# Three extra eight-row loads into unused buffers, early in a two-part decode-attention kernel

## The chip, the cores and the metric

The kernel runs on one core of a Trainium2 chip. The metric is device time in microseconds of one execution. Six executions of the kernel before took 1369.67 to 1370.08 us, with a median of 1369.79. One further execution was recorded by the hardware profiler; it took 1369.97 us, and its span, from its first to its last instruction, is 1368.20 us.

## The reference: what is computed

Two attention layers for one new token are computed side by side, each with its own input x (4 sequences, 512 wide), caches and weights, all in bf16. A uses 8 key/value heads for 32 query heads and only the last 2048 positions of its cache; B has 32 heads of each kind and uses all 8192 positions. The results are put side by side.

```python
q = (x @ wq).reshape(B, Sq, H, Dh).transpose(0, 2, 1, 3)
scores = einsum("bhqd,bhkd->bhqk", q, k) * (Dh ** -0.5)
o = einsum("bhqk,bhkd->bhqd", softmax(scores, axis=-1), v)
out = o.transpose(0, 2, 1, 3).reshape(B, Sq, H * Dh) @ wo
# A: k, v are the last 2048 of 8192 positions, each head used by 4 query heads
# result: concatenate([out_A, out_B], axis=-1)
```

There is one query row per sequence and head, so nearly all of the work is reading the caches: 587 MB come from memory in one execution.

## The kernel before

**Chunks.** The work is cut into 40 chunks. The first 8 belong to A, one per key/value head, with 2 MB of keys and 2 MB of values each. The other 32 belong to B, one per sequence and group of four heads, with 8 MB of keys and 8 MB of values each.

**The big buffer.** `kv` (line 229) holds ten units of 128 rows x 16 KB. While A runs, units 0 and 1 hold A's query weights, 6 and 7 B's query weights (`dma_wq`, line 337), 8 and 9 A's keys, 4 and 5 A's values (`dma_A`, line 361). Units 2 and 3 are used by nothing until B. In B, units 0 to 3 take keys and 4 to 7 values. Units 8 and 9 are a common second half: GpSimd copies the later half of a chunk's keys, and then of its values, there (`spread_copies`, line 369), so that the unit it came from is free for the next load. B's first chunk is an exception: `dma_K` (line 378) loads its keys' second half into units 8 and 9 directly, so units 2 and 3 are first written by the keys of B's second chunk.

**Compute.** TensorE transposes each block of 128 positions of the keys (line 477), VectorE and ScalarE take the transposed blocks out of PSUM into `kt` (lines 547 and 545), TensorE multiplies them with the queries (`sc`, line 479), ScalarE makes the exponentials (line 671), TensorE multiplies these with the values (`po`, line 479), and per chunk the output projection is added into `fin`.

**Order.** Nothing decides the order at run time. A recording object (`_Sched`, line 54) collects for each engine a list of instructions with the results each waits for; `add_dma` (line 78) gives every load a semaphore and a name. SyncE issues all big loads in the order of the lists (lines 457 to 469): query weights of A, first keys of A, query weights of B, then in each turn of A's loop the next keys, the values and a 512 KB block of A's output weights (`dma_wo`, line 346), then B's keys and values chunk by chunk. ScalarE issues the two loads of x (line 335). GpSimd issues no DMA at all; it sets constants, the last of them `back` (lines 312 to 316, named `c_back`), and later runs the copies of line 375.

**Freeing a buffer.** For each of the ten units, the list `held` (line 320) has the names of what must be over before the next load into it may be issued. `take` and `dma_K` read `held` for their waits and set it anew. Before the change, `held[2]` and `held[3]` are empty until B's first entries, so the keys of B's second chunk wait only for the releases of units 0 and 1.

Of the kernel before, what the change touches and what calls it, by code (L numbers as in the profile page):

```python
# [18 lines left out]
NWO = 3  # L19
# [153 lines left out]
def bass_concat_heads__sliding_block_cached__mha_block_cached__decode_kernel(  # L173
# [9 lines left out]
    KC = D // P  # L183
# [4 lines left out]
    WQ = {0: A_wq, 1: B_wq}  # L188
# [30 lines left out]
    sch = _Sched()  # L219
    with ExitStack() as es:  # L220
        block = es.enter_context(nc.Block())

        def sb(name, shape, dt):
            return es.enter_context(nc.sbuf_tensor(name, shape, dt))

        def ps(name, shape, dt):
            return es.enter_context(nc.psum_tensor(name, shape, dt))

        kv = sb("kv", [P, NH, 8192], BF16)
# [42 lines left out]
        semnames = ["eng_pe", "eng_dve", "eng_act", "eng_pool", "eng_sp", "d_x0", "d_x1", "d_o0", "d_o1", "r_k", "r_v", "r_w"]  # L272
        semnames += ["d_h%d" % i for i in range(NH)] + ["d_bk0", "d_bv0", "r_c"]
        semnames += [f + str(i) for f, x in (("d_lk", LASTK), ("d_nk", NEXTK), ("d_fk", HALVES), ("d_lv", LASTV), ("d_nv", NEXTV), ("d_hv", HALVES)) for i in range(len(x))]
        semnames += ["d_wo%d" % i for i in range(NWO)] + ["d_wos"]
        sems = {n: es.enter_context(nc.semaphore(n)) for n in semnames}


# [13 lines left out]
            waits=["c_onesf", "c_identf"], key="c_ind")  # L292
# [27 lines left out]
        held = [[] for _ in range(NH)]  # L320
# [10 lines left out]
        def flat(at, n):  # L331
            return kv[:, at:at + n, :].rearrange("p s x -> p (s x)")

        def dma_x(ab):
            sch.add_dma("act", lambda e: e.dma_start(xs[:, ab, :], X[ab][:, 0, :]), "d_x%d" % ab, key=("x", ab))
# [7 lines left out]
        def wo_slot(g):  # L343
            return g % 2 if g < NCA - 1 else 2

        def dma_wo(g):

            src = A_wo[g * 4 * P:(g + 1) * 4 * P, :].rearrange("(p r) n -> p (r n)", r=4)
            slot = wo_slot(g)
            dst = wor[:, slot, :]  # L350
            sch.add_dma("sp", lambda e: e.dma_start(dst, src), "d_wo%d" % slot,
                        waits=[("fin", g - 2)] if g >= 2 and slot < 2 else [], key=("wo", g))
# [8 lines left out]
        def dma_A(kind, c):  # L361
            ch = chunks[c]
            T = A_k if kind == "k" else A_v
            at = HALF_A[kind][c % 2]
            waits = take((kind, c), at, 1, ("T", ch["s_last"]) if kind == "k" else ("pv", c))
            src = T[:, ch["g"], SkA - W:, :].rearrange("b (pp j) d -> pp b (j d)", pp=P // NB)
            sch.add_dma("sp", lambda e: e.dma_start(kv[:, at, :], src), "d_h%d" % at, waits=waits, key=(kind, c))
# [86 lines left out]
        PIECES_K.update({NC - 5: ("d_fk", HALVES), NC - 4: ("d_fk", HALVES), NC - 3: ("d_fk", HALVES), NC - 2: ("d_nk", NEXTK)})  # L454
        PIECES_V = {NC - 3: ("d_hv", HALVES), NC - 2: ("d_nv", NEXTV), NC - 1: ("d_lv", LASTV)}

        dma_x(0)
        dma_x(1)
        dma_wq(0, 0)
# [2 lines left out]
        for c in range(NCA):  # L462
            if c < NCA - 1:
                dma_A("k", c + 1)
            dma_A("v", c)
            dma_wo(c)
        for c in range(NCA, NC):
            dma_K(c)
            dma_V(c)
# [553 lines left out]
```

## Time and profile before

| what | value |
|---|---|
| median of six executions | 1369.79 us |
| profiled execution, whole | 1369.97 us |
| profiled execution, span | 1368.20 us |
| time outside the span | 1.77 us |
| PE busy | 1198.4 us (88%) |
| VectorE, ScalarE, GpSimd busy | 776.5, 521.1, 470.4 us |
| read from memory | 587.21 MB, 429 GB/s over the span |
| packets of DMA queue 1 | 17432 |

How to read it: busy times are sums over the span and overlap each other. "DMA share" is the mean busy share of the core's 16 DMA engines; by rounding it can exceed 1. A load is cut into packets, which the DMA engines work off one after another, each engine on its own; a load has landed when the last of the engines that carry it is through. The trace holds, for each packet, its queue, start, duration and size, but not its engine, and for each landing signal its time; a 128-row load gives 16 such signals. All times are microseconds from the start of the span unless the text says ns.

### The profile page before, as it was taken

To read this page: it belongs to the slowest core of one execution; us is meant where nothing else is said; L and a number is where in the kernel's file an instruction comes from. 1 tells how busy PE (TensorE), PEld (TensorE's weight loads), DVE (VectorE), ACT (ScalarE), POOL (GpSimd) and SP (SyncE) were. 2 spreads that over 40 slices of the span, in tenths; PEclk is the share of its full clock that TensorE was granted. 3 is DMA by queue.
4 is the path that set the end of the run, shared out by engine and by line. 5 is a ranking of instruction groups with operands and counts; after the bars stand their busy time and mean duration, and the time that the engine had idled before them with its cause. 6 is when DMAs were issued, how large, how long until landed. Compare 5 with 4: busy or idle time off the path is not lost.

```text
span 1368.2 us, 61987 instructions
## 1 busy us (share of the span) xinstructions
PE 1198.4 (88%) x27577; PEld 1130.8 (83%) x27577; DVE 776.5 (57%) x1527; ACT 521.1 (38%) x681; POOL 470.4 (34%) x277
## 2 busy tenths in 40 slices
PE   4898698898989988988889888888998888998998
PEld 4787688887888988887889878888998888997897
DVE  1675455554556555555565655555665555665665
ACT  1553243333334433333344333333443333443443
POOL 2000244334433443344334433443344334432442
PEclk9899899999999999999999999999999999999999
DMA  9999999999999999999999999999999999999998
GB/s 400 426 426 439 433 428 433 429 441 429 429 431 434 436 433 429 435 437 431 433 435 439 425 433 441 435 424 433 443 433 433 425 443 431 433 425 428 426 425 353
DMA packets 17487, 587.54 MB, mean 429 GB/s; under 512 B 1956, under 2 KB 1976, under 8 KB 4408
## 3 DMA queue, kind: packets, MB, share of 16 engines
q1 hardware_dynamic: 17432, 587.21, 99.6%
q8 instruction: 15, 0.25, 0.1%
q14 instruction: 8, 0.07, 0.0%
q10 hardware_dynamic: 32, 0.01, 0.0%
HBM read 587.21 MB, written 0.01 MB: 429 GB/s over the span
## 4 chain that ended last, share of the span: by engine, by line
DMA 62%; PE 33%; DVE 2%; issue 1%; POOL 1%; ACT 0%; SPq 0%; POOLq 0%; DVEq 0%
DMA kv<-in_B_k_cache_dram 53%; PE tr L477 21%; PE sc L479 8%; DMA kv<-in_B_v_cache_dram 7%; PE fin L479 2%; DMA kv<-in_B_wq_dram 2%; POOL kv L375 1%; PE po L479 1%; DVE sA L601 1%; PE ms L479 1%; DVE rm L613 0%; DVE sA L599 0%; ACT pba L711 0%; PE ms L477 0%; DVE zA L802 0%
## 5 line engine op out<-in xcount | busy, mean ns | idle before, releaser
L477 PE MATMUL tr<-identb,kv 128*128 128x128 bf16 x8704 | 696.7, 227 | 110.1 <-POOLq L76 105.7
L375 POOL COPY kv<-kv 128x2048 int32<-128x2048 int32 x248 | 460.5, 1894 | 874.7 <-DMA kv<-in_B_k_cache_dram 308.3
L547 DVE COPY kt<-tr 128x1024 bf16<-128x1024 bf16 x736 | 503.6, 691 | 352.8 <-PE tr L477 350.0
L477 PEld LDWEIGHTS tr<-identb,kv 128*128 128x128 bf16 x8704 | 536.5, 102 | 127.7 <-issue 123.9
L545 ACT ACTIVATE kt<-tr 128x1024 bf16<-128x1024 bf16 x352 | 359.3, 1023 | 716.2 <-PE tr L477 716.0
L479 PE MATMUL sc<-qq,kt 128*128 128x64 bf16 x8192 | 404.5, 193 | 12.6 <-DVE kt L547 9.8
L479 PEld LDWEIGHTS sc<-qq,kt 128*128 128x128 bf16 x8192 | 338.7, 99 | 16.2 <-DVE kt L547 13.1
L479 PE MATMUL po<-pbb,kv 128*128 128x64 bf16 x8192 | 269.1, 194 | 16.7 <-POOLq L76 10.6
L479 PEld LDWEIGHTS po<-pbb,kv 128*128 128x128 bf16 x8192 | 259.5, 99 | 19.4 <-issue 14.0
L671 ACT ACTIVATE pbb<-sc,negb 32x128 bf16<-32x128 f32 x256 | 138.5, 541 | 6.6 <-DVE negb L649 1.8
L818 DVE CAST wor<-tr 128x512 bf16<-128x512 f32 x96 | 62.7, 681 | 0.7 <-PE sc L479 0.7
L617 DVE TENSOR_REDUCE rm<-sc 128x4 f32<-128x512 f32 x64 | 43.9, 686 | 14.3 <-PE sc L479 14.3
L687 DVE TENSOR_REDUCE hs<-pbb 128x4 f32<-128x512 bf16 x64 | 43.9, 686 | 10.4 <-ACT pbb L671 10.4
L683 ACT ACTIVATE hs<-hs 128x4 f32<-128x4 f32 x32 | 6.6, 205 | 105.3 <-DVE hs L679 105.3
L634 DVE TENSOR_REDUCE gm<-ms 4x4 f32<-4x128 f32 x72 | 24.0, 334 | 25.8 <-PE ms L477 25.8
L479 PE MATMUL tr<-wos,back 32*128 32x512 bf16 x384 | 34.5, 383 | 0.0
L479 PE MATMUL sc<-wos,back 32*128 32x512 bf16 x128 | 33.6, 382 | 0.0
L649 DVE TENSOR_SCALAR negb<-ms 128x4 f32<-128x4 f32 x64 | 10.4, 162 | 39.6 <-PE ms L479 39.6
L692 DVE TENSOR_TENSOR fd<-po,hs 128x64 f32<-128x64 f32 x32 | 7.2, 225 | 45.0 <-PE po L479 45.0
L765 DVE TENSOR_TENSOR hs<-ms,hs 128x4 f32<-128x4 f32 x32 | 5.2, 162 | 44.0 <-PE ms L479 44.0
L479 PE MATMUL fin<-wor,oz 128*4 128x256 bf16 x264 | 29.3, 365 | 0.4 <-DVE oz L790 0.4
L479 PE MATMUL sc<-qb,kt 128*128 128x64 bf16 (+3 forms) x512 | 26.1, 196 | 0.2 <-DVE gx L640 0.2
(74 smaller groups left out, 376.4 us busy)
## 6 DMA issues: line engine op xcount, KB each, us to landing
kv<-in_B_k_cache_dram SPq DMA_DIRECT2D x8, 4096.0 KB, 25.7
kv<-in_A_k_cache_dram SPq DMA_DIRECT2D x8, 2048.0 KB, 12.3
kv<-in_A_v_cache_dram SPq DMA_DIRECT2D x8, 2048.0 KB, 13.9
kv<-in_B_v_cache_dram SPq DMA_DIRECT2D x3, 4096.0 KB, 29.1
kv<-in_B_k_cache_dram SPq DMA_DIRECT2D x5, 2048.0 KB, 26.9
kv<-in_B_v_cache_dram SPq DMA_DIRECT2D x4, 2048.0 KB, 27.0
kv<-in_B_k_cache_dram SPq DMA_DIRECT2D x6, 1024.0 KB, 29.8
kv<-in_A_wq_dram SPq DMA_DIRECT2D x1, 4096.0 KB, 12.5
```

Source lines behind the costliest of these rows:

```text
L375: lambda e, x=x: e.tensor_copy(flat(KX, 2)[:, x].bitcast(I32), flat(units, 2)[:, x].bitcast(I32)),
L477: sch.add("pe", lambda e: e.transpose(o, l, r), waits, key)
L479: sch.add("pe", lambda e: e.matmul(o, l, r, start=start, stop=stop), waits, key)
L545: sch.add("act", lambda e: e.activation(dst, src, ACTF.Copy), waits=waits, key=("ev", s))
L547: sch.add("dve", lambda e: e.tensor_copy(dst, src), waits=waits, key=("ev", s))
L601: emit = lambda e, src=src, b=b: e.scalar_tensor_tensor(out=t, in0=src, scalar=mk[:, b:b + 1], in1=t, op0=ALU.mult, op1=ALU.add)
L617: sch.add("dve", lambda e: e.tensor_reduce(out=rm[:, half, :], in_=src, axis=AX.X, op=ALU.max), waits=[("S", ch["s"] + (half + 1) * ch["NG ...
L634: sch.add("dve", lambda e: e.tensor_reduce(out=gm[0:C, m, 0:U], in_=src, axis=AX.XY if B else AX.X, op=ALU.max), waits=[("trm", c, half)], ...
L649: sch.add("dve", lambda e: e.tensor_scalar(out=negb[:, m, 0:C], in0=ms[:, col:col + C], scalar1=-scale, scalar2=None, op0=ALU.mult), waits ...
L671: sch.add("act", lambda e, src=src, dst=dst, pp=pp, u=u: e.activation(dst, src, ACTF.Exp, bias=negb[pp, half, u:u + 1], scale=scale), wait ...
L687: sch.add("dve", lambda e: e.tensor_reduce(out=hs[:, half, :], in_=probs_B(half).rearrange("p j u -> p u j"), axis=AX.X, op=ALU.add), wait ...
L818: sch.add("dve", lambda e: e.tensor_copy(wol[:, u, :], o), waits=[("reord", c) if u == 3 else ("reord", c, u)] + [("fin", prev(c))], key=( ...
```

## The change

A view `probe` of B's query weights is made, 128 rows of 32 KB. Two loads are added to GpSimd's list, behind the last setup instruction, one to SyncE's list, in the turn c = 4 of A's loop, after that turn's block of output weights. Their targets lie in units 2 and 3, in rows that are 4 apart: the first load takes rows 0 to 28 of unit 2 (16 KB each), the second rows 64 to 92 of units 2 and 3 together (32 KB each), the third rows 1 to 29 of half of unit 2 (8 KB each). Nothing reads what they load. `held[2]` and `held[3]` name them, so that the keys of B's second chunk, which overwrite these units, wait for them. Three semaphores are added. Nothing is removed, and the lists of the other engines stay as they were.

```diff
-        semnames += ["d_wo%d" % i for i in range(NWO)] + ["d_wos"]
+        semnames += ["d_wo%d" % i for i in range(NWO)] + ["d_wos", "d_p0", "d_p1", "d_p2"]
...
+        probe = WQ[1].rearrange("(p r) n -> p (r n)", r=KC)
+        sch.add_dma("pool", lambda e: e.dma_start(kv[0:32:4, 2, :], probe[0:8, 0:8192]), "d_p0", waits=[("c_back", 3)], key="p0")
+        sch.add_dma("pool", lambda e: e.dma_start(flat(2, 2)[64:96:4, :], probe[8:16, :]), "d_p1", waits=[("c_back", 3)], key="p1")
+        held[2], held[3] = ["p0", "p1", "p2"], ["p1"]
         dma_x(0)
         dma_x(1)
         dma_wq(0, 0)
...
             dma_A("v", c)
             dma_wo(c)
+            if c == 4:
+                sch.add_dma("sp", lambda e: e.dma_start(kv[1:32:4, 2, 0:4096], probe[16:24, 0:4096]), "d_p2", key="p2")
```

## Prediction

> **What bounds the kernel now.** I read the DMA part of the page first, then a table of stages, then the chain of waits at the end, and last the trace's records of single DMA packets and of landings.
>
> The page's DMA parts:
>
> ```profile
> DMA  9999999999999999999999999999999999999998
> GB/s 400 426 426 439 433 428 433 429 441 429 429 431 434 436 433 429 435 437 431 433 435 439 425 433 441 435 424 433 443 433 433 425 443 431 433 425 428 426 425 353
> ...
> q1 hardware_dynamic: 17432, 587.21, 99.6%
> q8 instruction: 15, 0.25, 0.1%
> q14 instruction: 8, 0.07, 0.0%
> ```
>
> The 16 DMA engines are full in every slice but the last, and queue 1, into which SyncE issues the loads, holds 99.6% of their time. A table of stages says the same with PE beside it (columns: length, then the busy time of PE, PE's weight loads, VectorE, ScalarE and GpSimd, each with its instructions, then PE's clock, DMA share, GB/s):
>
> ```profile
> 68.00:102.00 34.00, 31.08 (x669) 27.49 (x670) 25.38 (x73) 18.59 (x29) 0.00 (x0) 1.00 1.01 428
> 209.70:248.40 38.70, 34.31 (x802) 32.51 (x802) 22.27 (x42) 14.77 (x19) 14.87 (x8) 0.96 1.00 434
> 1340.00:1354.00 14.00, 13.69 (x333) 13.50 (x331) 9.92 (x17) 7.93 (x10) 5.56 (x3) 1.00 1.02 433
> 1354.00:1368.20 14.20, 9.82 (x249) 8.10 (x244) 5.83 (x16) 2.37 (x5) 0.00 (x0) 1.00 0.60 247
> ```
>
> The DMA share is 1.00 while PE has 34.31 us of work in a 38.70 us chunk. The chain of waits over the last microseconds (start, length, what) names what the end hangs on:
>
> ```profile
> 1351.62 0.25 PE sc L479 x8
> 1352.02 0.43 SPq L432
> 1352.50 0.43 SPq L432
> 1352.97 11.44 DMA kv<-in_B_v_cache_dram
> 1364.51 0.42 PE po L479 x8
> 1365.28 0.62 PE fin L479 x8
> 1365.99 0.42 DVE outsb L850
> ```
>
> The last piece of V lands at 1364.41, and 3.8 us of fixed work follow. So the span is "when the slowest of 16 DMA engines is through its bytes", plus 3.8 us. What matters is not the mean engine but the slowest.
>
> The packet records give each engine's pace. A 64 KB packet takes 2.420 us, one of 32 KB 1.213, 16 KB 0.611, 8 KB 0.309, 4 KB 0.159, nearly without spread. The landing records give the order of the engines: in each big load 16 landings are recorded. At 13.35 us the first engine is 0.77 us ahead of the last; at 100.34 seven engines lead by 1.42 to 2.18 us and nine lie within 0.93 of the last; at 212.21 seven lead by 2.92 to 3.74 and seven lie within 0.72; at 1364.41 the first leads by 2.64. The gap does not close by itself, because no engine waits for another. What opens it are the 15 packets of queue 8 (instruction fetches, 16 KB, recorded at 0.98 to 1.11 us each, from 18.6 to 173.2 us): each sets one engine back by about 1 us.
>
> **The change part by part.** It adds three loads and removes nothing; the order on PE, VectorE and ScalarE is the same.
>
> *Load 1* (Pool queue): eight rows of 16 KB. *Load 2* (Pool queue): eight rows of 32 KB. *Load 3* (SyncE): eight rows of 8 KB. In all 448 KB. The nearest row for how rows go to engines is the load of x: four rows of 1 KB each left four 1 KB packets on queue 10, so a row stays whole and goes to one engine. Per engine that is hit: load 1 0.611 us, load 2 1.213, load 3 0.309, by the packet rows above.
>
> GpSimd issues its two after its last setup instruction:
>
> ```profile
> 8.52 2.97 POOL L314 TENSOR_SCALAR_AFFINE_SELECT back<-back 128x512 bf16<-128x512 bf16 x4
> ```
>
> that is at about 11.5 us. Behind them on GpSimd stand only the relays and copies of the B part, whose first busy slice is after 137 us, so GpSimd's own issuing time, which no row shows, is covered by some 120 us. SyncE's load stands between its issues at 78.02 and 78.39:
>
> ```profile
> 78.02 0.33 SPq L351 DMA_DIRECT2D wor<-in_A_wo_dram  x1
> 78.39 0.54 SPq L367 DMA_DIRECT2D kv<-in_A_k_cache_dram  x1
> ```
>
> It delays the K load behind it by one issue, 0.33 to 0.54 us. The engines are then still busy with the load issued at 78.02, which lands at 84.45; a new load's packets start some 2.2 us after its issue (343.46 to 345.7 in the records), so more than 3 us of cover remain. The new wait of the B part's second K load, which SyncE issues at 133.52, is over long before: the first two loads should land before 20 us, the third at about 85. That wait costs nothing; without that cover every load behind it on SyncE would move.
>
> What remains is engine time, and that has no cover on an engine that is already the last. A load that hits the last engine moves the end by its full packet time; on an engine that leads by more than the packet time it costs nothing. So the sum is bounded by 0 below (only leaders are hit) and by 0.611 + 1.213 + 0.309 = 2.13 us above, if the Pool queue's packets run at queue 1's pace. If the 448 KB were spread evenly it would be 28 KB an engine, 1.06 us.
>
> Which engines are hit is the first choice. The trace does not name engines, but it shows which four carry a four-row transfer. At 126.9 us the output of A interrupts four engines; following their packets to 129.3, they lead the last one by about 3.4, 3.4, 2.6 and 2.1 us at 134.49. So four of the engines that a small transfer uses here are leaders. I therefore place load 3 (eight rows, from SyncE) on leaders, at nothing. For the Pool queue no row exists. I take it that the two Pool loads do not both go to the same eight engines, since their target rows (0 to 28 and 64 to 92) lie in different halves of the memory; then one of them hits the last engine. I take the larger, 1.2 us; the smaller would give 0.6.
>
> [...]
>
> The second choice is the pace of the Pool queue. Low end: queue 1's, 0.611 us for 16 KB; queue 14's 8 KB fetches, at 0.307 to 0.325, agree. High end: queue 8's 16 KB packets, up to 1.11 us. I take queue 1's, because it is the only one of these with rows into the same buffers.
>
> [...]
>
> **Sum.** Span 1368.20 + 1.2 = 1369.4. The profiled execution took 1369.97, 1.77 more than its span, and the median is 1369.79, 0.18 less than it: 1369.4 + 1.77 - 0.18 = 1371.0.
>
> **The rivals.**
>
> *Leaders only* (1369.8): all three loads fall on engines that lead. The early leads are 1.42 to 2.18 us, later 2.9 and more, against at most 2.13 us of load. For it: the four known engines lead. Against it: nothing says that Pool's loads use the same ones.
>
> *Piled on the last engines* (1371.9): all three on the half that has the fetches, +2.13. Against it: the four known engines.
>
> *Slower*: the Pool queue's packets run at queue 8's pace because a second queue on a full engine loses its turn: 3 x 1.07 + 0.31 = 3.5 us on the engines that carry all three, 1373.3. It decides once 16 KB cost over 0.81 us there (3 x 0.81 + 0.31 = 2.74 us, which is 0.2%). For it: 15 rows of exactly such a case, a 16 KB packet on another queue beside a full queue 1. Against it: queue 14 does not show it. A first use of the Pool queue may also cost time outside the span, where 1.77 us lie today; no row tells.
>
> *Faster*: setting the leading engines back changes how the engines meet, and the gap shrinks. The most that could bring is the first engine's lead at the end, 2.64 us, and nothing makes the last engine's bytes fewer; I give it -1 us, 1368.8.
>
> **How the numbers follow.** Forecast (one Pool load on the last engine, +0.6 to +1.3) 0.40; leaders only (0 to +0.3) 0.25; piled (+1.8 to +2.1) 0.11; slower (+2.8 to +3.6) 0.22; faster 0.02. A difference under 0.2%, 2.74 us, is about what a measurement of this kernel can tell from no change. The first three cases lie within it: 0.76. The slower case is beyond: 0.22; and 0.02 for faster, at the very most. The first three hold less than 8 in 10, so the range takes in the slower one: 1369.7 to 1373.4.
>
> **What would show it.** In the changed kernel's packet records: 8 packets (or pieces) of 16 and of 32 KB on a new queue from about 12 us, at 0.611 and 1.213 us, or longer for the slower rival. In the landing records after 20 us: the lead of the first engines grows by 1.2 us if the last ones are hit, and shrinks if the leaders are. The last V landing moves by the same amount as the span, and the 3.8 us after it stay. The forecast is wrong if the period of 38.70 us a chunk changes, if GpSimd is late at its first copy, or if the time outside the span grows.

## The result, and the profile after

The changed kernel takes 1373.03 us (median of 20 runs, 1372.66 to 1373.59), the kernel before 1369.83 us (40 runs). The ratio is 1.0023, with a 95% interval of 1.0017 to 1.0029: 3.20 us slower. The forecast was +1.2 us; the time lies in the range, at the place of the slower rival. The profiled execution took 1373.09 us, 1371.4 of them in the span, so the time outside the span stayed at 1.7 us.

The end of the chain of waits, after (start, length, what):

```profile
1355.09 0.43 SPq L432
...
1355.57 0.43 SPq L432
...
1356.04 11.47 DMA kv<-in_B_v_cache_dram
...
1367.61 0.42 PE po L485 x8
...
1368.37 0.62 PE fin L485 x8
...
1369.08 0.42 DVE outsb L856
```

It is the same chain, later. The last piece of V lands at 1367.51 in place of 1364.41, 3.10 us later, and the tail behind it is as long as it was. Nothing was added at the end; the DMA engines come to it late. Where the time was lost is read from a table of stages (length, busy time of PE, PE's weight loads, VectorE, ScalarE, GpSimd with their instructions, PE's clock, DMA share, GB/s). From 17 to 22 us, before:

```profile
17.00:22.00 5.00, 3.76 (x46) 3.77 (x47) 1.16 (x3) 1.94 (x2) 0.00 (x0) 1.00 1.05 449
```

The same stretch, after:

```profile
17.00:22.00 5.00, 0.71 (x7) 0.72 (x8) 0.26 (x2) 0.00 (x0) 0.00 (x0) 1.00 1.05 341
```

The last two columns are what to look at. The DMA share is 1.05 in both, but the engines move 341 GB/s in place of 449. Both columns count a packet whole in the window in which it starts. That, and not rounding, is why the share can exceed 1, and it makes the rate of so short a window scatter: it is 423 in the run with the third load alone, where nothing differs from before at this time. If of each packet only the part that lies in the window is counted, from the packet records, the share is 1.00 to 1.01 in every run of this document, and the rate is 428 GB/s before and 324 after. Over 5 us that is 0.52 MB too few, which at 428 GB/s are 1.2 us. A busy share of 100% did not mean full speed here. Rates "by parts" below are counted in this second way.

The queues, after:

```profile
q1 hardware_dynamic: 17448, 587.28, 99.5%
q0 software_dynamic: 64, 0.39, 0.1%
q8 instruction: 15, 0.25, 0.1%
```

Queue 0 is new; it carries the two Pool loads, 0.39 MB. Its packet records say what the shares do not. The eight 16 KB packets start from 15.62 to 16.48 us and take 0.611 us each, as foretold. The eight 32 KB packets start from 17.45 to 18.06 us and take 1.76 to 2.24 us, 2.03 on average, where queue 1's packets of that size take 1.213. Beside them, 24 packets of queue 1 that start from 17.33 to 20.36 us take 1.37 to 2.09 us as well (one more long packet, of 1.71 us at a code fetch, is in before too). At 20.37 us 16 packets of queue 1 are under way at once, one for each engine, and all of them are long, though the last packet of the second load ended at 20.30. No engine was spared.

What the two issuers did, after; GpSimd first, then SyncE:

```profile
11.80 0.69 POOL L458 DMA_DIRECT2D kv<-in_B_wq_dram  x1 [0.30 <-POOL back L314]
12.49 0.52 POOL L459 DMA_DIRECT2D kv<-in_B_wq_dram  x1
```

```profile
77.67 0.33 SPq L351 DMA_DIRECT2D wor<-in_A_wo_dram  x1
78.05 0.77 SPq L472 DMA_DIRECT2D kv<-in_B_wq_dram  x1
78.87 0.58 SPq L367 DMA_DIRECT2D kv<-in_A_k_cache_dram  x1
```

Both issue when the prediction said. SyncE's third load takes 0.77 us to issue, more than the 0.33 and 0.58 of its neighbours, under the same cover.

### The profile page after: what moved, and what is told of

Same layout as the page of the kernel before. It is cut to its first block, busy times and chain, and to the rows that moved or that the text cites. A ratio compares the mean times of both kernels' runs of the same rounds, so it can differ in the third digit from the quotient of the medians.

```text
span 1371.4 us, 61992 instructions
## 1 busy us (share of the span) xinstructions
PE 1195.7 (87%) x27577; PEld 1128.0 (82%) x27577; DVE 776.9 (57%) x1527; ACT 521.1 (38%) x681; POOL 471.5 (34%) x279
## 4 chain that ended last, share of the span: by engine, by line
DMA 63%; PE 34%; DVE 1%; POOL 1%; issue 1%; SPq 0%; ACT 0%; POOLq 0%; DVEq 0%
DMA kv<-in_B_k_cache_dram 52%; PE tr L483 21%; PE sc L485 8%; DMA kv<-in_B_v_cache_dram 5%; DMA kv<-in_A_k_cache_dram 3%; PE fin L485 2%; DMA kv<-in_B_wq_dram 2%; PE po L485 2%; POOL kv L375 1%; PE ms L485 1%; DVE sA L607 0%; PE tr L485 0%; PE ms L483 0%; ACT pba L717 0%; DVE kt L553 0%
```

## The experiments

Three theories were put against each other. **A**: the price is set by which engines carry a load and into which rows they write; the second Pool load is dear because its rows 64 to 92 are usually written by other engines (an assumption of the theory: no record names the engine that wrote a row). **B**: the Pool queue as such is dear. **C**: the bytes alone count. In the table, "own rows" means that the second load writes rows 2 to 30 (2 to 14 where it has four), beside rows 0 to 28 and 1 to 29 of the other two loads; other targets are called foreign below. Both are names for target rows and say nothing of engines. The difference is between the medians of the run's kernel and of the kernel before, taken together. The ratio's intervals are about 0.0009 to each side for most runs, wide beside the smaller differences: for six runs they take in 1, so these differences rest on the medians with their spread and on the packet records. All kernels are variants of the changed one; none leaves out a part of the attention itself. In the last column before has 428.

| run | median, us (spread) | difference | ratio [95%] | GB/s by parts, 17 to 22 us |
|---|---|---|---|---|
| third load alone (p2_only) | 1369.88 (1369.74 to 1370.81) | -0.01 | 1.0000 [0.9991, 1.0009] | 428 |
| first alone (p0_only) | 1370.17 (1369.95 to 1370.39) | +0.28 | 1.0000 [0.9991, 1.0009] | 428 |
| first and third (p0_p2) | 1370.39 (1370.26 to 1370.59) | +0.51 | 1.0003 [0.9994, 1.0012] | 428 |
| second alone, own rows (p1_own_only) | 1370.71 (1370.58 to 1371.12) | +0.83 | 1.0006 [0.9997, 1.0015] | 428 |
| all, second in own rows (p1_own) | 1371.64 (1371.41 to 1371.78) | +1.75 | 1.0011 [1.0002, 1.0020] | 428 |
| second alone (p1_only) | 1372.04 (1371.90 to 1373.53) | +2.15 | 1.0015 [1.0006, 1.0024] | 357 |
| the change | 1373.03 (1372.66 to 1373.59) | +3.20 | 1.0023 [1.0017, 1.0029] | 324 |
| first two by ScalarE (act_queue) | 1373.12 (1372.64 to 1373.42) | +3.27 | 1.0022 [1.0013, 1.0031] | 313 |
| second in rows 32 to 39 (p1_rows32) | 1375.19 (1374.72 to 1375.99) | +5.37 | 1.0040 [1.0026, 1.0054] | 202 |
| second as 16 rows (p1_rows16) | 1372.21 (1371.97 to 1372.53) | +2.39 | 1.0017 [1.0008, 1.0027] | 330 |
| four rows, own (four_own) | 1371.05 (1370.98 to 1371.34) | +1.20 | 1.0008 [0.9999, 1.0017] | 428 |
| four rows, rows 64 to 76 (four_other) | 1372.41 (1372.18 to 1372.58) | +2.56 | 1.0017 [1.0008, 1.0026] | 339 |
| 448 KB evenly (even) | 1370.95 (1370.77 to 1371.10) | +1.10 | 1.0007 [0.9998, 1.0016] | 427 |

### One load at a time

For the first load alone, the lines of the second and third are removed; the others likewise, with `held` cut to match.

```diff
-        sch.add_dma("pool", ... flat(2, 2)[64:96:4, :], probe[8:16, :] ... "d_p1" ...)
-        held[2], held[3] = ["p0", "p1", "p2"], ["p1"]
+        held[2], held[3] = ["p0"], []
...
-            if c == 4:
-                sch.add_dma("sp", ... "d_p2", key="p2")
```

> Only the first Pool load (8 rows of 16 KB into rows 0 to 28) is kept. The changed kernel is 3.2 us slower than before. Theory A (other half's rows): the cost comes from the second Pool load, whose rows 64 to 92 are the ones that the other eight engines write; this first load runs at 0.611 us a packet, on engines that lead, so 0 to +0.3 us, 1369.8 to 1370.1. Rival B (Pool queue as such): each use of it costs the same, about half of the change, +1.5 us, 1371.3. Rival C (bytes alone, piled on eight engines of which one is the last): +0.6 us, 1370.4.

Measured +0.28 us, packets at 0.611 us. Theory A's range holds it. Theory B falls: a Pool load can be nearly free. Theory C's 0.6 is too much.

> Only the second Pool load (8 rows of 32 KB into rows 64 to 92) is kept. Theory A: its packets take 1.8 to 2.2 us where queue 1's 32 KB take 1.213, the packets of all engines beside it take up to 2.1 us too, and the end moves by 1.3 to 2.0 us, 1371.1 to 1371.8. Rival B: +1.5 us as for the other Pool load, 1371.3, with the first load alone costing as much. Rival C: packets at 1.213 us, +1.2 us at most, 1371.0.

Measured +2.15 us, a little above theory A's range; the eight packets take 1.77 to 2.28 us with no other Pool load before them, and the 428 GB/s of before become 357 (329 from 15.3 to 20.3 us, since this load's packets start 1.7 us earlier than in the changed kernel). So the long packets belong to this load and not to there being two.

> Only SyncE's load (8 rows of 8 KB into rows 1 to 29, in the turn c = 4) is kept. Theory A and rival B: without the Pool loads the engines that it hits lead, so 0 to +0.1 us, 1369.8 to 1369.9. Rival C: +0.31 us, 1370.1. If SyncE's issue of 0.77 us or the new wait mattered: +0.5 us or more, 1370.3.

Measured -0.01 us: no change. Neither SyncE's longer issue nor the new wait costs anything that can be seen.

### The second load's rows

```diff
-        sch.add_dma("pool", lambda e: e.dma_start(flat(2, 2)[64:96:4, :], probe[8:16, :]), "d_p1", ...)
+        sch.add_dma("pool", lambda e: e.dma_start(flat(2, 2)[2:32:4, :], probe[8:16, :]), "d_p1", ...)
```

> All three loads, but the second Pool load writes rows 2 to 30 in steps of 4 in place of 64 to 92; bytes, queue and time of issue are the same. Theory A: its packets take 1.21 us in place of 2.0, the other eight engines are not slowed, and of the 3.2 us 1.2 to 1.8 go: +1.4 to +2.0 us, 1371.2 to 1371.8. Rivals B and C: nothing changes, 1373.0.

Measured +1.75 us: 1.45 of the 3.20 us go with the row numbers alone. The stages, for this kernel:

```profile
17.00:22.00 5.00, 1.98 (x19) 1.98 (x20) 0.43 (x2) 0.91 (x1) 0.00 (x0) 1.00 1.08 459
```

The 459 GB/s are 428 by parts, as before the change. All eight 32 KB packets take 1.213 us, and no packet of queue 1 is long but the one at a code fetch. Source, bytes, queue and issue time are the changed kernel's; only the target differs. Rivals B and C, which expected no change, fall for this part.

### The queue

```diff
-        sch.add_dma("pool", ... "d_p0", ...)
-        sch.add_dma("pool", ... "d_p1", ...)
...
         dma_x(1)
+        sch.add_dma("act", ... "d_p0", ...)
+        sch.add_dma("act", ... "d_p1", ...)
```

> The two Pool loads are issued by ScalarE, behind its loads of x and with the same wait, so that no load uses the Pool queue; bytes, rows and target rows are the changed kernel's. Theory A (the rows that a load writes, and the engines that carry it, set the price): the 32 KB packets again take 1.8 to 2.2 us and the end moves by 2.8 to 3.4 us, 1372.6 to 1373.2. Rival B (Pool queue as such): the cost goes, 0 to +1 us, 1369.8 to 1370.8.

Measured +3.27 us, with the 32 KB packets at 1.78 to 2.29 us. This kernel's queues in the same 5 us:

```profile
q1 hardware_dynamic: 63, 1.43, 83.9%
q10 hardware_dynamic: 21, 0.26, 21.3%
q8 instruction: 1, 0.02, 1.7%
```

Queue 10, ScalarE's, has taken the place of queue 0, and its 32 KB packets are as long. The Pool queue is not the cause.

### The same bytes, spread evenly

```diff
-        sch.add_dma("pool", ... "d_p0", ...)
-        sch.add_dma("pool", ... "d_p1", ...)
-        held[2], held[3] = ["p0", "p1", "p2"], ["p1"]
+        sch.add_dma("pool", lambda e: e.dma_start(kv[:, 2, 0:1792], probe[:, 0:1792]), "d_p0", waits=[("c_back", 3)], key="p0")
+        held[2], held[3] = ["p0"], []
```

SyncE's load is left out as well.

> The same 448 KB go in one Pool load over all 128 rows (3.5 KB a row, 28 KB for each engine), the other two loads are left out. Theory A: every engine gets 1.1 us of work and writes only its usual rows, so +1.0 to +1.3 us, 1370.9 to 1371.2, whatever the leads are. Rival B: one use of the Pool queue, +1.5 us on top or alone, 1371.4 to 1372.5. Rival C (bytes on the last engine): +1.1 us as theory A.

Measured +1.10 us against 1.06 for 28 KB an engine, an estimate from the 1.213 us of 32 KB. I read it so: with the same bytes on every engine no lead was used, and the full price was paid; it is a third of the change's.

### Four rows: on engines that lead?

```diff
-        ... kv[0:32:4, 2, :], probe[0:8, 0:8192] ...  flat(2, 2)[64:96:4, :], probe[8:16, :] ...
+        ... kv[0:16:4, 2, :], probe[0:4, 0:8192] ...  flat(2, 2)[2:16:4, :], probe[8:12, :] ...
-        ... kv[1:32:4, 2, 0:4096], probe[16:24, 0:4096] ...
+        ... kv[1:16:4, 2, 0:4096], probe[16:20, 0:4096] ...
```

The first two come from ScalarE, as above; the second of these runs has rows 64:80:4 in place of 2:16:4.

> All three loads with four rows in place of eight (224 KB in all), the first two issued by ScalarE, the second into rows 2 to 14: per engine the same bytes as in the run with the second load's rows moved, which was 1.75 us slower than before, but on four engines only, those that carry x and lead by about 2 us and more in the trace of before. Theory A (an engine that leads takes its load for nothing): 0 to +0.2 us, 1369.8 to 1370.1. Rival C (the price is the packet time wherever it falls): +1.75 us, 1371.6.

Measured +1.20 us. Theory A as I applied it missed: I had taken all four engines for leaders. Of the 2.13 us of packet time on each of them, 0.93 was free. The landing records show how the last engine comes about. At 51.36 us it is one of a group of eight within 0.65 us; a code fetch starts at 50.94 and takes 1.07, and at 57.26 one engine alone is 1.26 us behind all others. If one of the four takes a fetch like this, it carries its loads on top. That would explain the cost, but it is not shown: the records name no engines, and a chain of packets joined by their starts and ends can jump from one engine to another where two end together. Rival C's 1.75 missed too.

> As the run with four rows, but the second load writes rows 64 to 76. The engines that carry it still lead. Theory A: the 32 KB that arrive in rows of other engines hold up those engines, which are among the last ones, so +0.6 to +1.4 us, 1370.4 to 1371.2, and packets of queue 1 longer than 1.3 us appear at about 16 to 22 us. If only the carrying engine pays: 0 to +0.2 us, 1369.8 to 1370.1.

Measured +2.56 us, above theory A's range, which was built on the wrong leads; against its twin it is +1.36, within what I had given to the rows. The stages of the twin with rows 2 to 14, then of this kernel:

```profile
17.00:22.00 5.00, 2.12 (x21) 2.12 (x22) 0.21 (x2) 1.05 (x2) 0.00 (x0) 1.00 1.04 446
17.00:22.00 5.00, 1.06 (x11) 1.07 (x12) 0.20 (x2) 0.00 (x0) 0.00 (x0) 1.00 1.06 364
```

22 of queue 1's packets from 17.3 to 20.0 us are longer than 1.3 us. At 19.94 us 15 of them are under way at once, far more than the four rows that the load writes. The surcharge for foreign rows is 1.36 with four rows and 1.45 with eight: from four to eight it hardly grows with the number of rows, when these are 4 apart.

### What makes rows foreign

```diff
-        ... flat(2, 2)[64:96:4, :], probe[8:16, :] ...
+        ... flat(2, 2)[32:40, :], probe[8:16, :] ...
```

for the first, and `kv[2:128:8, 3, :], probe[8:24, 0:8192]` for the second.

> As the changed kernel, but the second Pool load writes the eight neighbouring rows 32 to 39 in place of 64 to 92: the lower half of the rows, like rows 2 to 30, which cost 1.75 us in all with packets of 1.213 us. Theory A1 (what costs is that engines of one half write rows of the other half): packets of 1.213 us, +1.75 us, 1371.6. [...]

Measured +5.37 us. The stages of this kernel:

```profile
17.00:22.00 5.00, 0.00 (x0) 0.00 (x0) 0.23 (x2) 0.00 (x0) 0.00 (x0) 1.00 1.21 229
```

The rate of 229 GB/s, 202 by parts, is the lowest of all; PE has nothing to do for 5 us. The share of 1.21 does not mean busier engines: by parts it is 1.01, and the rest is long packets that start in the window and end behind it. The packets take 2.92 to 4.41 us. Rows 32 to 39 lie in the lower half, so it is not the half that counts: A1, with packets of 1.213 us and +1.75, falls.

> As the changed kernel, but the second Pool load has 16 rows of 16 KB, rows 2, 10, ... 122, the same 256 KB over both halves. If a row goes to an engine in order, each engine gets one row of its own half, but mostly one that another engine of that half usually writes. Theory A1 (other half): packets of 0.611 us and nothing else slowed; 0.611 for each engine on top of the other two loads, +1.0 to +1.4 us, 1370.8 to 1371.2. [...]

Measured +2.39 us, with packets of 0.611 to 1.16 us. A1's +1.4 at most, with no packet above 0.611, falls here too.

### The price of own rows

The second Pool load alone, into rows 2 to 30; then the changed kernel without its second load.

```diff
-        sch.add_dma("pool", ... "d_p0", ...)
-        sch.add_dma("pool", lambda e: e.dma_start(flat(2, 2)[64:96:4, :], probe[8:16, :]), "d_p1", ...)
+        sch.add_dma("pool", lambda e: e.dma_start(flat(2, 2)[2:32:4, :], probe[8:16, :]), "d_p1", ...)
```

> Only the second Pool load, into rows 2 to 30. So far the loads into rows of their own engines gave: 0.31 us of packet time 0, 0.61 us +0.28, 2.13 us +1.75. Theory A (the price is the packet time less some 0.35 us, the lead that the last of the eight engines has): 1.21 - 0.35 = +0.86 us, 1370.7. Rival C (the full packet time once it is over some size): +1.2 us, 1371.05. Rival D (a share of it, 1.75/2.13): +1.0 us, 1370.85.

Measured +0.83 us.

> The changed kernel without its second Pool load: 0.92 us of packet time on eight engines, all into their own rows. Theory A: 0.92 - 0.35 = +0.57 us, 1370.4. Rival C: +0.92 us, 1370.75. Rival D: +0.76 us, 1370.6. Beside the changed kernel (+3.2) it tells what the second Pool load adds to the other two: 2.6 us by theory A, over twice its 1.21 us.

Measured +0.51 us. Both fit theory A within 0.06 us. With the earlier runs, five packet times of eight-row loads into own rows, which I take to be on the same eight engines, 0.31, 0.61, 0.92, 1.21 and 2.13 us, cost -0.01, 0.28, 0.51, 0.83 and 1.75: the first is covered whole, and each of the others is the packet time less 0.33 to 0.41 us. I read that as the lead of the last of the eight engines. The landings of before fit: at 1364.41 the three engines next to the last lead it by 0.27, 0.42 and 0.44 us.

## Why the prediction was right in its range and wrong in its likeliest case

**What bounds the kernel.** Right: the span moved with the last landing, +3.10 us of +3.2.

**The loads' packet times.** Load 1: 0.611 us, right. Load 3: 0.309 us for seven of its eight packets, right. Load 2: foretold 1.213, measured 2.03 on average. This is the term that was mis-sized, and more than its own size was missing from the sum: the other engines' packets became longer too. With own rows it is 1.213 to the nanosecond.

**The covers.** Right. GpSimd's issuing of 1.2 us, SyncE's of 0.77 and the new wait cost nothing: the third load alone changes nothing, and the first alone costs 0.28 us, less than its packet time.

**Which engines are hit.** "I take it that the two Pool loads do not both go to the same eight engines": wrong. In the changed kernel, in seven of the eight cases a 32 KB packet starts 1.827 us after a 16 KB one, to within 0.001, which is three times the 16 KB packet's time (the packet itself and two of queue 1's of that size), and in the eighth 1.225, twice it. So I take them for the same eight engines, and the costs agree: into own rows the second load adds its whole packet time to what the other two cost. The reason I gave, that the target rows lie in different halves, did not hold by this: the rows did not choose the engines. That these engines then wrote rows which others usually write is my estimate of the trouble and was not shown; what was shown is that the second load took 1.213 us a packet into rows 2 to 30 and 2.03 into rows 64 to 92.

**The leads.** That a load on a leading engine is free is right in kind: of each total of eight-row loads into own rows 0.31 to 0.41 us was free (the smallest, 0.31, whole). But I read the leads of four engines and took them for the group's. One engine with little lead is enough to be the last.

**The third load.** Placed on leaders at nothing. Alone it is free. In the changed kernel the eight had no lead left. The load issued just before it lands at 87.02, 2.57 us later than before, and the one issued behind it at 92.22, 2.88 us later: the third load cost its full 0.31.

**The sum as it came out.** Loads 1 and 3 together +0.51; load 2 into own rows adds 1.24, its packet time; its foreign rows add 1.45: 3.20.

**The rivals.** "Slower" had the size, 3.5 us, and the wrong mechanism: queue 8's pace is not a second queue's pace, since the same bytes on the same queue into other rows ran at 1.213 us. "Piled on the last engines" came nearest in kind, with the eight engines right in part and the rows unseen. "Faster" and "leaders only" did not happen. So the range held by luck: it reached up to 1373.4 only for a mechanism that did not occur, and the cost that did occur, that of the target rows, stands nowhere in the sum.

**What stays open.** Why some rows are dear. The records name neither the engine of a packet nor what it waited for, so the runs show the cost by target (all three loads: +1.75 us with the second in rows 2 to 30, +2.39 as 16 rows, +3.20 in rows 64 to 92, +5.37 in rows 32 to 39) and not its cause. And why every engine loses that time. With four foreign rows, twelve engines lead by 2.94 to 3.38 us when A's first keys land (20.89 us), and ten microseconds later eleven of them by 1.7 to 2.1: they lost about 1.2 us, although the load writes only four rows.

## What to carry to other kernels

Where all DMA engines are full, look for the engine that is last, engine by engine, before pricing a small load: for eight-row loads into own rows, 0.31 us of packet time cost nothing here, and 0.61 to 2.13 us cost all but 0.33 to 0.41, which I read as the smallest lead among the engines that carry them. Measure the target rows as well: the same 256 KB cost 1.45 us more in rows 64 to 92 than in rows 2 to 30, and 3.62 more in rows 32 to 39, and from 17 to 22 us the 16 engines together moved 324 and 202 GB/s in place of 428. And read the DMA share together with GB/s: by parts the engines were full from 17 to 22 us in every variant (1.00 to 1.01), and the dearest moved half the bytes in that time (202 GB/s in place of 428).

## What the runs showed of the hardware that I had not expected

A load of 256 KB slowed all 16 engines together from 428 to 324 GB/s for 5 us by its target rows alone, and to 202 GB/s when eight rows lay side by side (by parts). It made no difference whether GpSimd or ScalarE issued it (+3.20 and +3.27 us). And delays of single engines did not average out: with four own rows one engine was alone behind by 1.26 us at 57.26 us, and at the last landing, 1365.47, two engines are 1.33 us behind all others.
